# In the seventh attention turn GpSimd takes the low part of h ahead of the product with z; in the eighth VectorE makes w1's low parts ahead of the denominators

## The chip, the cores and the metric

One core of a Trainium2 chip runs the whole kernel as one launch. The metric is device time in microseconds (us) of that launch. The kernel before takes 517.39 us (median of 3 runs, 517.29 to 517.85).

## The reference

A transformer-like block over 2048 tokens of width 512, in float32. First comes linear attention with 32 heads of width 16, whose queries and keys pass through a small matrix per head and then a softmax of both signs; then a token-mixing MLP with 1792 hidden units that works along the token axis.

```python
qkv = layernorm(x) @ wqkv                                  # 32 heads of 16
pq, pk = per-head q @ w_phi, k @ w_phi
phi_q = concat(softmax(pq), softmax(-pq))
phi_k = concat(softmax(pk), softmax(-pk))
kv = sum over s of phi_k^T v ;  z = sum over s of phi_k
o = (phi_q kv) / (phi_q z + 1e-6)
h = x + o @ wo
n = layernorm(h)
u = gelu(einsum("sd,sf->df", n, w1) + b1)                  # w1: 2048 x 1792
out = h + einsum("df,fs->sd", u, w2) + b2                  # w2: 1792 x 2048
```

## The kernel before, in words

The tokens are cut into 16 tiles of 128. Matrix products that need float32 accuracy are made of three matmuls: each operand is split into a high part (rounded copy, made by ScalarE) and a low part (operand minus high part, made by VectorE or GpSimd), and `mm3` issues high by high (line 68), high by low (line 69) and low by high (line 70).

After keys and values are done, a loop of 20 turns (`for it in range(NT + 4)`, line 715) runs the query side of attention as a software pipeline, with the first two column pairs of the MLP's first product (`fills`, line 698) between its steps, so that TensorE always has something to do. Within the loop the order on TensorE, VectorE, ScalarE and GpSimd is the order in which the code is written; the queue of SyncE, which issues the loads, is ordered by a scheduler. An engine works its list strictly in order. The first turn is `it = 0`, so the seventh is `it = 6` and the eighth `it = 7`. What a turn does, by helper:

- `s_pq(it+1)` (GpSimd, line 473): multiplies the softmax numerators `eq` of a query tile by their weights `w`.
- `s_ez(it+3)` (GpSimd, line 457): `ez = eq * zB`, the product with z, which the denominators of that tile need.
- `s_den(it+2)` (VectorE, lines 466 to 470): sums `ez` per head into `tz`, combines it with the softmax sums `smq`, and ends in the weights `w` (line 470), which `s_pq` of the next turn uses.
- `q_sums` (VectorE, line 230): the softmax sums `smq` of one further query tile.
- `s_tr`, `s_num`, `s_wo` (TensorE lines 547, 566 and 68 to 70 with `po`): transposes, numerators and the product with wo. ScalarE copies the results out as `pht` (line 549) and `oh` (line 572), and VectorE makes `ol` (line 577).
- `s_h(it-2)` (VectorE, line 594): adds x, giving a tile of `h`.
- `s_moments`, `s_rstd`, `s_hn(it-4)` (ScalarE lines 603 to 605, GpSimd line 610 as `r`, ScalarE lines 613 to 63): the second layer norm. The last gives `hs`, whose high part ScalarE copies (line 63) and whose low part GpSimd subtracts (line 64). These are the names `hs<-hb,hs` in the profile.
- `fills(it)` (TensorE, lines 68 to 70 with `pu<-hs`): in turn `it` it first takes tile `it-6` of `hs` with column pair 1 of w1, then tile `it-5` with column pair 0, six matmuls each. The second and the fifth of the six (line 69) read the low part of `hs`, the third and the sixth (line 70) the low part of w1.
- `flush` (VectorE, line 664): makes the low parts `wlo` of those pieces of w1 whose high parts ScalarE has made (line 670). They wait in the list `LATER` until a `flush` comes.

The lines of a turn around the change:

```python
        if it < NT:
            s_x(it)
        if it + 3 < NT:
            s_ez(it + 3)
        negate()
        q_mm()
        fills(it)
        q_exp(0)
        logits = q_logits(1)
        if it >= 4 and even:
            s_hn(it - 4)
        ...
        run(logits + (q_sums(0) if it > 0 else []), den)
        ...
        if 0 <= it - 2 < NT:
            s_h(it - 2)
        flush()
```

`run` issues its two lists alternately. `negate` and `logits` have nothing left to do in the turns spoken of here, the logits of all 16 query tiles having been made before.

Of the kernel before, what the change touches and what calls it, by code (L numbers as in the profile page):

```python
# [19 lines left out]
NT = S // P  # L20
# [9 lines left out]
Q_AT = (4, 6, 8, 9, 11, 13)  # L30
V_NOT = (0, 1, 11)
SUMS = 8
DEN_EPS = 1e-6
LAG = 5
WARM = 9
# [4 lines left out]
def block_kernel(ctx: ExitStack, tc: tile.TileContext, x, xT, wT, phic, wo, w1, b1, w2, b2,  # L40
# [17 lines left out]
    nc.vector.memset(eps2[:, :1], EPS * EPS)  # L58
    nc.vector.memset(eps2[:, 1:], DEN_EPS / 2)

    def split(hi, lo, src, lo_engine):

        nc.scalar.activation(hi, src, AF.Copy)  # L63
        lo_engine.tensor_sub(lo, src, hi)  # L64
# [16 lines left out]
    ps_s = px.enter_context(tc.tile_pool(name="ps_s", bufs=1, space=PSUM, side="right"))  # L81
    sums = ps_s.tile([P, SUMS, NPR, 2, 2], F32, name="smq")
    wqp = aq.enter_context(tc.tile_pool(name="wqp", bufs=1, side="right"))
# [93 lines left out]
    def turns(*lists):  # L177

        return [ops[i] for i in range(max(map(len, lists))) for ops in lists if i < len(ops)]

    def run(*lists):
        for op in turns(*lists):
            op()
# [4 lines left out]
    def heads(e):  # L188
        return e.rearrange("p g (a d) -> p (g a) d", d=DH)
# [36 lines left out]
    def q_sum(t):  # L226

        assert t < SUMS or t - SUMS in W, "a tile's sums would go where others are still wanted"
        SQ[t] = sums[:, t % SUMS]
        return [lambda: nc.vector.reduce_sum(SQ[t].rearrange("p g c h -> p (g c h)"), heads(EQ[t]), axis=AX.X)]  # L230
# [144 lines left out]
    def q_mm():  # L375
        if q["mm"] < NT:
            PS[q["mm"]] = proj(q["mm"], wqh, wql, ps_q, "pu")
            q["mm"] += 1

    def q_logits(lag):  # L380
        n = q["logits"]
        if n < min(NT, q["mm"] - lag + NT * (q["mm"] == NT)):
            EQ[n] = big.tile([P, NG, P], F32, name="eq", tag="big")
            q["logits"] += 1
            return logit_ops(PS[n], EQ[n], n >= len(Q_AT))
        return []
# [7 lines left out]
    def q_sums(lag):  # L394
        n = q["sum"]
        if n < min(NT, q["exp"] - lag + NT * (q["exp"] == NT)):
            q["sum"] += 1
            return q_sum(n)
        return []
# [55 lines left out]
    def s_ez(t):  # L455
        EZ[t] = az.tile([P, NG, P], F32, name="ez")
        nc.gpsimd.tensor_mul(EZ[t], EQ[t], zB)  # L457

    def s_den(t):


        tz = az.tile([P, NPR, 2, 2], F32, name="tz")
        den = az.tile([P, NPR, 2], F32, name="den")
        W[t] = az.tile([P, NPR, 2, 2], F32, name="w", bufs=3)
        other = SQ[t][:, :, ::-1]
        return [lambda: nc.vector.reduce_sum(tz.rearrange("p g c h -> p (g c h)"), heads(EZ[t]), axis=AX.X),
                lambda: nc.vector.tensor_mul(tz, other, tz),
                lambda: nc.vector.reduce_sum(den, tz.rearrange("p g c h -> p g h c"), axis=AX.X),
                lambda: nc.vector.reciprocal(den, den),
                lambda: nc.vector.tensor_mul(W[t], other, den.unsqueeze(2).to_broadcast([P, NPR, 2, 2]))]  # L470

    def s_pq(t):
        nc.gpsimd.tensor_mul(heads(EQ[t]), heads(EQ[t]), W[t].rearrange("p g c h -> p (g c h)").unsqueeze(2).to_broadcast([P, 2 * H, DH]))  # L473
# [54 lines left out]
    def keep(shape, dt, name, i):  # L528
        return keep_pool.tile(shape, dt, name=name, tag=f"keep{i}")
# [11 lines left out]
    def s_tr(t):  # L541
        j, i = divmod(t, 2)
        if i == 0:
            PHT[j] = ak.tile([P, NG, 2, P], F32, name="pht", bufs=1)
        ptr = ps_t.tile([P, 2, 4, P], F32, name="tn")
        for g in range(NG):
            nc.tensor.transpose(ptr[:, g // 4, g % 4, :], EQ[t][:, g, :], ident)  # L547
        for half in range(2):
            nc.scalar.activation(PHT[j][:, half * 4:half * 4 + 4, i, :], ptr[:, half], AF.Copy)  # L549

    def s_kv():

        pt = ps_o.tile([P, 2, P], F32, name="po")
        for b in range(2):
            nc.tensor.transpose(pt[:, b, :], kvS[:, 2 * b:2 * b + 2, :].rearrange("p n f -> p (n f)"), ident)
        nc.scalar.activation(kvB, pt, AF.Copy)

    def s_num(j):


        pn = ps_t.tile([P, 2, 4, P], F32, name="tn")
        for b in range(2):
            for c in range(4):
                for r in range(2):
                    rows, cols = slice(64 * r, 64 * r + 64), slice(32 * c, 32 * c + 32)
                    nc.tensor.matmul(pn[cols, r, 2 * b:2 * b + 2, :], kvB[rows, b, cols], PHT[j][rows, 4 * b + c, :, :],
                                     start=True, stop=True, skip_group_check=True)
        oh = ak.tile([P, 2, 2, 2, P], F32R, name="oh", bufs=1)
        ol = ak.tile([P, 2, 2, 2, P], F32R, name="ol", bufs=1)
        pv = pn.rearrange("p r (b i) s -> p i r b s", i=2)  # L570
        for i in range(2):
            nc.scalar.activation(oh[:, i], pv[:, i], AF.Copy)
        OS[j] = oh, ol, pv
# [35 lines left out]
    def s_rstd(t):  # L609
        nc.gpsimd.tensor_tensor(r2[:, t:t + 1], VE[t][:, 0:1], mhalf[:, :1], op=ALU.pow)  # L610

    def s_hn(t):
        nc.scalar.activation(VE[t][:, 1:2], VE[t][:, 1:2], AF.Copy, scale=r2[:, t:t + 1])
        i, k = divmod(t, 2)
        if i not in HB:
            if i == 7:
                HB[i] = hb7
            else:
                both = keep([P, 2, 4, HD], F32, "hb", i // 2)
                BOTH[i // 2] = both  # L620
                HB[i], HB[i + 1 - i // 6] = both[:, 0], both[:, 1 - i // 6]
        hn = HB[i][:, 2 * k:2 * k + 2].rearrange("p h d -> p (h d)")
        nc.scalar.activation(hn, HT[t], AF.Identity, scale=r2[:, t:t + 1], bias=VE[t][:, 1:2])
        HN[t] = big.tile([P, 2, D], F32R, name="hs", tag="big")
        split(HN[t][:, 0], HN[t][:, 1], hn, nc.gpsimd)
# [35 lines left out]
    def flush():  # L661
        while LATER:
            wl_, raw, wh_ = LATER.pop(0)
            LO.append(nc.vector.tensor_sub(wl_, raw, wh_).ins)
# [42 lines left out]
    def t_at(it, place):  # L707
        for op in T_AT.get((it, place), "").split():
            i = int(op[1])
            if op[0] in "hl":  # L710
                (t_hi if op[0] == "h" else t_lo)(i)
            else:
                t_sums(i, "abcd".index(op[0]))

    for it in range(NT + 4):
        even = it % 2 == 0
        t_at(it, 0)
        if 0 <= it + 1 < NT:
            s_pq(it + 1)
        if it == 0:  # L720
            s_tr(0)
            s_kv()
        if it == 1:
            run(q_logits(0))
            q_mm()
            s_tr(1)
        if it > 1 and even and it <= NT:
            s_num(it // 2 - 1)
        t_at(it, 1)
        den = s_den(it + 2) if it + 2 < NT else []  # L730
        if it > 1 and even and it <= NT:
            ol = s_ol(it // 2 - 1)
            run(ol[:1] + den[:1] + ol[1:])
            den = den[1:]
        if it < NT:
            s_x(it)
        if it + 3 < NT:
            s_ez(it + 3)
        negate()
        q_mm()  # L740
        fills(it)
        q_exp(0)
        logits = q_logits(1)
        if it >= 4 and even:
            s_hn(it - 4)
        if 3 <= it < NT + 3 and even:
            s_moments(it - 3)
        if it > 1 and even and it - 2 < NT:
            s_wo(it - 2)
        if 1 < it < NT:  # L750
            s_tr(it)
        if it > 1 and not even and it - 2 < NT:
            s_wo(it - 2)
        if it >= 4 and not even:
            s_hn(it - 4)
        if 3 <= it < NT + 3 and not even:
            s_moments(it - 3)
        if 3 <= it < NT + 3:
            s_rstd(it - 3)
        run(logits + (q_sums(0) if it > 0 else []), den)  # L760
        if it > 0:
            negate()
        if not logits:
            flush()
        t_at(it, 2)
# [3 lines that stand above are left out]
        t_at(it, 3)  # L769
        if it > NT + 1:  # L770
            fill_load(2)
        for p in range(2):
            if it >= LAG - 3 + p and FL[p] <= FN[p] + 2 * (FN[p] > 0):
                fill_load(p)
# [488 lines left out]
```

## Time and profile before

| | |
|---|---|
| median of 3 runs | 517.39 us (517.29 to 517.85) |
| the profiled execution's own time | 516.99 us |
| its span in the profile | 515.2 us |
| TensorE matmul busy | 509.3 us, 99% of the span |
| TensorE weight load busy | 439.3 us, 85% |
| VectorE busy | 445.9 us, 87% |
| ScalarE busy | 297.2 us, 58% |
| GpSimd busy | 244.6 us, 47% |
| TensorE clock granted | 1.00 |

The profile is of one execution. A row of its timeline gives the start in us from the beginning of the span, the duration, engine, line, operation, output and inputs; a bracket at the end gives the idle time of the engine before the row and what ended it. PE is TensorE, DVE VectorE, ACT ScalarE, POOL GpSimd. Consecutive instructions overlap a little, so the spacing of starts tells what an instruction costs its engine. In the 20 us from 180 to 200, which hold the seventh, eighth and part of the ninth turn, TensorE is busy for 18.85 us, VectorE for 18.15, ScalarE for 15.02 and GpSimd for 19.44; in the 20 us ahead of them and the 20 behind them TensorE is busy throughout.

### The profile page before, as it was taken

What the parts mean: (1) busy time and instruction counts of PE and PEld (TensorE: products, weight loads), DVE (VectorE), ACT (ScalarE), POOL (GpSimd) and SP (SyncE); (2) the same over time, 40 slices, a digit from 0 to 9 for tenths busy, and PEclk for the clock granted to TensorE, in tenths of its full rate; (3) what the DMA queues carried; (4) which work ended last, traced back from release to release, by engine and by line L of the source; (5) the groups of instructions that cost most, each with busy time, mean ns of one, the idle gap of its engine ahead of it and who ended that gap; (6) DMA issues with size and microseconds to landing.
All of it is one profiled execution on the core that took longest, in us unless ns stands there. A gap on an engine that the chain in (4) does not pass through costs nothing.

```text
span 515.2 us, 9360 instructions
## 1 busy us (share of the span) xinstructions
PE 509.3 (99%) x3546; PEld 439.3 (85%) x3546; DVE 445.9 (87%) x765; ACT 297.2 (58%) x494; POOL 244.6 (47%) x188
## 2 busy tenths in 40 slices
PE   8999999999999999999999999999999999999997
PEld 8888888887877778777788899998888898899897
DVE  6793999986789998777796998989989899998985
ACT  6998954525245876668976643457753444444430
POOL 2579799984999999975343300000002212211220
PEclk9999999999999999999999999999999999999999
DMA  8844311000041324333322333374135688667833
GB/s 315 268 124 123 83 45 39 1 1 2 22 145 41 103 83 142 124 123 123 112 93 83 83 104 104 101 245 137 47 123 127 161 184 165 148 140 194 166 44 78
DMA packets 36300, 58.56 MB, mean 114 GB/s; under 512 B 3744, under 2 KB 19360, under 8 KB 36256
## 3 DMA queue, kind: packets, MB, share of 16 engines
q1 hardware_dynamic: 31648, 50.85, 31.5%
q0 software_dynamic: 4032, 6.42, 9.5%
q8 instruction: 28, 0.46, 0.4%
q10 hardware_dynamic: 576, 0.69, 0.4%
q14 instruction: 16, 0.13, 0.1%
HBM read 46.81 MB, written 11.14 MB: 112 GB/s over the span
## 4 chain that ended last, share of the span: by engine, by line
PE 94%; POOL 3%; ACT 1%; DVE 1%; issue 0%; POOLq 0%
PE py L1105 20%; PE pu L935 12%; PE pu L68 8%; PE pu L69 8%; PE pu L70 8%; PE py L1109 7%; PE pv L69 3%; PE pv L70 3%; PE pv L68 3%; PE pk_ps L68 3%; PE pk_ps L69 2%; PE pk_ps L70 2%; PE tn L547 2%; PE po L70 2%; PE po L69 2%; PE po L68 2%
## 5 line engine op out<-in xcount | busy, mean ns | idle before, releaser
L1181 POOL DMA_DIRECT2D out<-ot x7 | 6.2, 885 | 157.7 <-DVE ot L1177 157.7
L991 ACT ACTIVATE whi<-wraw 128x1792 fp32r<-128x1792 f32 x28 | 47.6, 1702 | 44.2 <-DVE wraw L858 26.6
L1001 DVE TENSOR_TENSOR wlo<-wraw,whi 128x1792 fp32r<-128x1792 f32 x28 | 56.6, 2020 | 4.9 <-PE py L1109 4.7
L1105 PE MATMUL py<-uf,whi 128*128 128x512 f32 x210 | 57.6, 393 | 0.0
L69 PE MATMUL pu<-hs,whi 128*128 128x512 f32 x128 | 50.3, 393 | 1.2 <-POOL hs L64 1.2
L68 PE MATMUL pu<-hs,whi 128*128 128x512 f32 x128 | 50.1, 399 | 0.0
L70 PE MATMUL pu<-hs,wlo 128*128 128x512 f32 x128 | 47.9, 390 | 0.0
L896 ACT ACTIVATE whi<-wraw 128x896 fp32r<-128x896 f32 x24 | 22.9, 955 | 31.2 <-PE pu L935 26.2
L457 POOL TENSOR_TENSOR ez<-eq,zB 128x1024 f32<-128x1024 f32 x16 | 38.3, 2396 | 4.5 <-ACT zB L502 4.5
L1105 PEld LDWEIGHTS py<-uf,whi 128*128 128x128 f32 x210 | 35.8, 189 | 4.3
L1105 PEld LDWEIGHTS py<-uf,wlo 128*128 128x128 f32 x210 | 33.1, 190 | 4.6
L935 PE MATMUL pu<-ht,whi 128*128 128x256 f32 x192 | 35.6, 283 | 0.0
L1105 PE MATMUL py<-uf,wlo 128*128 128x256 f32 x210 | 34.9, 280 | 0.0
L210 POOL TENSOR_TENSOR pk<-pk,sk 128x1024 f32<-128x1024 f32 x16 | 31.0, 1941 | 6.3 <-DVE sk L209 6.3
L64 POOL TENSOR_TENSOR hs<-hb,hs 128x512 fp32r<-128x512 f32 x16 | 22.3, 1393 | 24.4 <-ACT hs L63 24.3
L549 ACT ACTIVATE pht<-tn 128x512 f32<-128x512 f32 x32 | 17.4, 596 | 28.6 <-PE tn L547 28.4
L473 POOL TENSOR_TENSOR eq<-eq,w 128x1024 f32<-128x1024 f32 x16 | 32.2, 2013 | 0.8 <-DVE w L470 0.8
L214 POOL TENSOR_TENSOR zacc<-zacc,pk 128x1024 f32<-128x1024 f32 x13 | 31.2, 2402 | 0.6
L186 ACT ACTIVATE pk<-pk,r 128x1024 f32<-128x1024 f32 x16 | 18.3, 1146 | 21.1 <-DVE pk L164 21.1
L68 PEld LDWEIGHTS pu<-hs,whi 128*128 128x128 f32 x128 | 24.0, 188 | 7.1 <-issue 2.5
L935 PEld LDWEIGHTS pu<-ht,whi 128*128 128x128 f32 x192 | 30.0, 192 | 0.0
L69 PEld LDWEIGHTS pu<-hs,whi 128*128 128x128 f32 x128 | 24.1, 188 | 6.6 <-POOL hs L64 2.1
(208 smaller groups left out, 1606.6 us busy)
## 6 DMA issues: line engine op xcount, KB each, us to landing
wraw<-in_w SPq DMA_DIRECT2D x28, 512.0 KB, 4.2
wraw<-in_w SPq DMA_DIRECT2D x48, 256.0 KB, 2.8
xraw<-in_xT SPq DMA_DIRECT2D x16, 256.0 KB, 3.0
xh<-in_x SPq DMA_DIRECT2D x16, 256.0 KB, 2.7
h<-in_x SPq DMA_DIRECT2D x16, 256.0 KB, 2.8
out<-h SPq DMA_DIRECT2D x14, 256.0 KB, 2.7
out<-ot POOLq DMA_DIRECT2D x14, 256.0 KB, 4.9
wraw<-in_wT SPq DMA_DIRECT2D x12, 256.0 KB, 5.1
```

Of the source, the lines that this page charges most:

```text
L68: nc.tensor.matmul(o, ah, bh, start=first, stop=False)
L69: nc.tensor.matmul(o, ah, bl, start=False, stop=False)
L70: nc.tensor.matmul(o, al, bh, start=False, stop=last)
L210: nc.gpsimd.tensor_mul(heads(PK[t]), heads(PK[t]), sk.unsqueeze(2).to_broadcast([P, 2 * H, DH]))
L214: nc.gpsimd.tensor_add(zacc, zacc, PK[t])
L457: nc.gpsimd.tensor_mul(EZ[t], EQ[t], zB)
L473: nc.gpsimd.tensor_mul(heads(EQ[t]), heads(EQ[t]), W[t].rearrange("p g c h -> p (g c h)").unsqueeze(2).to_broadcast([P, 2 * H, DH]))
L935: nc.tensor.matmul(ACC[p][bk][:, half], WS[p, i][x][:, a], hb[b][y], start=i == 0 and half == 0 and k == 0, stop=i == NT // 2 - 1 and k == ...
L991: nc.scalar.activation(WH[g], RAW[g], AF.Copy)
L1001: nc.vector.tensor_sub(wl_, RAW[g], WH[g])
L1105: nc.tensor.matmul(o, w, u, start=p == 0 and not low, stop=p == NP - 1, skip_group_check=True)
L1109: nc.tensor.matmul(bank[bk][:, half], AW[sp, p][x][:, a], UB[p, b][:, y], start=p == 0 and half == 0 and i == 0, stop=p == NP - 1 and i == ...
```

## The change

It swaps two steps on GpSimd in the seventh turn and puts two steps of VectorE earlier in the eighth. No instruction is added or removed.

```diff
+TURN = 6
...
-        if it + 3 < NT:
+        if it + 3 < NT and it != TURN:
             s_ez(it + 3)
         negate()
         q_mm()
...
         if it >= 4 and even:
             s_hn(it - 4)
+        if it == TURN:
+            s_ez(it + 3)
         if 3 <= it < NT + 3 and even:
             s_moments(it - 3)
...
         if 3 <= it < NT + 3:
             s_rstd(it - 3)
+        if it == TURN + 1:
+            run(q_sums(0))
+            flush()
         run(logits + (q_sums(0) if it > 0 else []), den)
```

On GpSimd, in the seventh turn and the one after it: `eq_1571` is query tile 7, `ez_2223` (after: `ez_2243`) the product with z for tile 9, `hs_2242` (after: `hs_2240`) the low part of h's tile 2, `hs_2341` that of tile 3; `eq_1619` and `eq_1773` are query tiles 8 and 9. The list before:

```order
L473 TENSOR_TENSOR eq_1571<-eq_1571,w_2123 128x1024
L457 TENSOR_TENSOR ez_2223<-eq_1773,zB_1536 128x1024
L64 TENSOR_TENSOR hs_2242<-hb_2071,hs_2242 128x512
L610 TENSOR_TENSOR r2_68<-ve2_2185,mhalf_63 128x1
L473 TENSOR_TENSOR eq_1619<-eq_1619,w_2217 128x1024
L457 TENSOR_TENSOR ez_2300<-eq_1785,zB_1536 128x1024
L64 TENSOR_TENSOR hs_2341<-hb_2071,hs_2341 128x512
```

And after, where the numbers of the lines are one higher from the new constant on:

```order
L474 TENSOR_TENSOR eq_1571<-eq_1571,w_2123 128x1024
L65 TENSOR_TENSOR hs_2240<-hb_2071,hs_2240 128x512
L458 TENSOR_TENSOR ez_2243<-eq_1773,zB_1536 128x1024
L611 TENSOR_TENSOR r2_68<-ve2_2185,mhalf_63 128x1
L474 TENSOR_TENSOR eq_1619<-eq_1619,w_2217 128x1024
L458 TENSOR_TENSOR ez_2300<-eq_1785,zB_1536 128x1024
L65 TENSOR_TENSOR hs_2341<-hb_2071,hs_2341 128x512
```

Only the second and the third row have changed places; what follows, and every later turn, is as it was.

On VectorE, in the eighth turn: `h_2049` is the last step of the seventh, `smq` the softmax sums (of query tile 11 from `eq_1838`, of tile 12 from `eq_1900`), `tz_2295` to `w_2297` the denominators of tile 9, `wlo_2286` and `wlo_2291` the low parts of two pieces of w1, `h_2124` the turn's last step, `ol_2384` (after: `ol_2385`) the first of the ninth turn. Before:

```order
L594 SCALAR_TENSOR_TENSOR h_2049,ve2_2281<-po_2249,h_2049 128x512
L230 TENSOR_REDUCE smq_83<-eq_1838 128x64
L466 TENSOR_REDUCE tz_2295<-ez_2223 128x64
L467 TENSOR_TENSOR tz_2295<-smq_83,tz_2295 128x64
L468 TENSOR_REDUCE den_2296<-tz_2295 128x32
L469 RECIPROCAL den_2296<-den_2296 128x32
L470 TENSOR_TENSOR w_2297<-smq_83,den_2296 128x64
L664 TENSOR_TENSOR wlo_2286<-wraw_2284,whi_2285 128x512
L664 TENSOR_TENSOR wlo_2291<-wraw_2289,whi_2290 128x512
L594 SCALAR_TENSOR_TENSOR h_2124,ve2_2357<-po_2326,h_2124 128x512
L577 TENSOR_TENSOR ol_2384<-tn_2366,oh_2383 128x512
```

After:

```order
L595 SCALAR_TENSOR_TENSOR h_2049,ve2_2281<-po_2249,h_2049 128x512
L231 TENSOR_REDUCE smq_83<-eq_1838 128x64
L665 TENSOR_TENSOR wlo_2286<-wraw_2284,whi_2285 128x512
L665 TENSOR_TENSOR wlo_2291<-wraw_2289,whi_2290 128x512
L231 TENSOR_REDUCE smq_83<-eq_1900 128x64
L467 TENSOR_REDUCE tz_2295<-ez_2243 128x64
L468 TENSOR_TENSOR tz_2295<-smq_83,tz_2295 128x64
L469 TENSOR_REDUCE den_2296<-tz_2295 128x32
L470 RECIPROCAL den_2296<-den_2296 128x32
L471 TENSOR_TENSOR w_2297<-smq_83,den_2296 128x64
L595 SCALAR_TENSOR_TENSOR h_2124,ve2_2358<-po_2326,h_2124 128x512
L578 TENSOR_TENSOR ol_2385<-tn_2367,oh_2384 128x512
```

The two low parts stand ahead of the denominators, and since `q_sums` now runs twice in this turn, the sums of tile 12 come into it from the ninth; every later turn's sums come one turn earlier too, until the 16 tiles are used up. On TensorE and ScalarE nothing changes its place.

On SyncE, the scheduler puts two loads the other way round: `wraw_2616` (after: `wraw_2617`) is a piece of w1, `h_2298` the tile of x to which the tenth turn adds, `out_0` a store of h. Before:

```order
L596 DMA out_0<-h_2049 128x512
L669 DMA wraw_2523<-in_w1 128x2x256
L588 DMA h_2298<-in_x 128x512
L669 DMA wraw_2616<-in_w1 128x2x256
L596 DMA out_0<-h_2124 128x512
```

After:

```order
L597 DMA out_0<-h_2049 128x512
L670 DMA wraw_2524<-in_w1 128x2x256
L670 DMA wraw_2617<-in_w1 128x2x256
L589 DMA h_2298<-in_x 128x512
L597 DMA out_0<-h_2124 128x512
```

The load of w1 now stands ahead of the load of x.

## The prediction

> **What bounds the kernel now.** I read the page's chain first, then TensorE's waits.
>
> ```profile
> PE 94%; POOL 3%; ACT 1%; DVE 1%; issue 0%; POOLq 0%
> ```
>
> ```profile
> PE pu L69 <- POOL hs L64: 1.2, 1, 1.2
> ...
> PE po L70 <- DVE ol L577: 0.2, 1, 0.2
> ```
>
> TensorE is the bound: the chain that ended last is 94% TensorE. Once started, it waits long only once (columns: total, times, longest), for GpSimd's low part of h, so only that wait is to be won; what GpSimd or VectorE gain elsewhere is worth nothing by itself. TensorE's timeline shows the place, the eighth turn, and three later rows that I need as marks.
>
> ```profile
> 185.96 0.39 PE L68 MATMUL pu<-hs,whi 128*128 128x512 f32 x1
> 187.50 0.50 PE L69 MATMUL pu<-hs,whi 128*128 128x512 f32 x1 [1.15 <-POOL hs L64]
> 187.84 0.40 PE L70 MATMUL pu<-hs,wlo 128*128 128x512 f32 x1
> ...
> 194.06 0.39 PE L70 MATMUL pu<-hs,wlo 128*128 128x512 f32 x1
> ...
> 195.20 0.39 PE L69 MATMUL pu<-hs,whi 128*128 128x512 f32 x1
> 195.43 0.39 PE L70 MATMUL pu<-hs,wlo 128*128 128x512 f32 x1
> ...
> 201.76 0.39 PE L70 MATMUL pu<-hs,wlo 128*128 128x512 f32 x1
> ```
>
> Undisturbed matmuls start 0.23 us apart (195.20 to 195.43). After 185.96 the L70 would have started at 186.42; it started at 187.84. The wait costs **1.42 us**, more than the 1.15 in the bracket, since the pipeline has to fill again. That is the most the change can bring.
>
> GpSimd's timeline through these turns, two pieces of one list:
>
> ```profile
> 181.49 1.94 POOL L473 TENSOR_TENSOR eq<-eq,w 128x1024 f32<-128x1024 f32 x1
> 183.39 2.38 POOL L457 TENSOR_TENSOR ez<-eq,zB 128x1024 f32<-128x1024 f32 x1
> 185.73 1.72 POOL L64 TENSOR_TENSOR hs<-hb,hs 128x512 fp32r<-128x512 f32 x1
> 187.41 0.54 POOL L610 TENSOR_TENSOR r<-ve,mhalf 128x1 f32<-128x1 f32 x1
> 187.93 1.93 POOL L473 TENSOR_TENSOR eq<-eq,w 128x1024 f32<-128x1024 f32 x1
> 189.82 2.39 POOL L457 TENSOR_TENSOR ez<-eq,zB 128x1024 f32<-128x1024 f32 x1
> 192.69 1.81 POOL L64 TENSOR_TENSOR hs<-hb,hs 128x512 fp32r<-128x512 f32 x1 [0.48 <-ACT hs L63]
> 194.47 0.54 POOL L610 TENSOR_TENSOR r<-ve,mhalf 128x1 f32<-128x1 f32 x1
> 194.98 1.94 POOL L473 TENSOR_TENSOR eq<-eq,w 128x1024 f32<-128x1024 f32 x1
> 196.88 2.41 POOL L457 TENSOR_TENSOR ez<-eq,zB 128x1024 f32<-128x1024 f32 x1
> 199.24 1.28 POOL L64 TENSOR_TENSOR hs<-hb,hs 128x512 fp32r<-128x512 f32 x1
> 200.48 1.00 POOL L610 TENSOR_TENSOR r<-ve,mhalf 128x1 f32<-128x1 f32 x1
> ```
>
> The reader is to see that GpSimd has almost no gap: it is full here. The low part of tile 2 ends at 187.45 and TensorE's L70 follows 0.39 us behind it. The next two, of tiles 3 and 4, end at 194.50 and 200.52; with the same 0.39 their L70 could start at 194.89 and 200.91, and start at 195.43 and 201.76. So TensorE can come forward by only 0.54 and 0.85 us before it meets GpSimd again, unless these low parts come earlier too. This, not the 1.42, decides.
>
> VectorE and ScalarE in the same stretch:
>
> ```profile
> 184.40 1.92 DVE L664 TENSOR_TENSOR wlo<-wraw,whi 128x512 fp32r<-128x512 f32 x1
> 186.24 0.68 DVE L594 SCALAR_TENSOR_TENSOR h<-po,h 128x512 f32<-128x512 f32 x1
> ...
> 186.85 1.22 DVE L230 TENSOR_REDUCE smq<-eq 128x64 f32<-128x1024 f32 x1
> 187.98 1.21 DVE L466 TENSOR_REDUCE tz<-ez 128x64 f32<-128x1024 f32 x1
> ...
> 190.12 0.22 DVE L470 TENSOR_TENSOR w<-smq,den 128x64 f32<-128x64 f32 x1
> 190.26 3.10 DVE L664 TENSOR_TENSOR wlo<-wraw,whi 128x512 fp32r<-128x512 f32 x2
> 193.28 0.68 DVE L594 SCALAR_TENSOR_TENSOR h<-po,h 128x512 f32<-128x512 f32 x1
> ...
> 195.41 0.69 DVE L577 TENSOR_TENSOR ol<-tn,oh 128x512 fp32r<-128x512 f32 x1 [1.44 <-ACT oh L572]
> ...
> 200.04 1.03 DVE L664 TENSOR_TENSOR wlo<-wraw,whi 128x512 fp32r<-128x512 f32 x1
> ```
>
> ```profile
> 181.84 0.63 ACT L63 ACTIVATE hs<-hb 128x512 fp32r<-128x512 f32 x1
> ...
> 185.75 1.15 ACT L670 ACTIVATE whi<-wraw 128x512 fp32r<-128x512 f32 x2
> ...
> 189.83 1.09 ACT L549 ACTIVATE pht<-tn 128x512 f32<-128x512 f32 x2 [1.89 <-PE tn L547]
> ...
> 191.98 0.63 ACT L63 ACTIVATE hs<-hb 128x512 fp32r<-128x512 f32 x1
> ...
> 194.31 1.07 ACT L572 ACTIVATE oh<-tn 128x512 fp32r<-128x512 f32 x2
> ```
>
> A low part of w1 and GpSimd hold each other up. The one issued at 184.40 goes through only when GpSimd's running product is over: VectorE's next instruction starts at 186.24, 0.51 us after GpSimd's boundary at 185.73. GpSimd's instruction behind that boundary then takes 1.72 instead of 1.28; likewise the r at 200.48, 1.00 instead of 0.54. So a low part costs GpSimd about 0.45 us. For two in a row the nearest place is another pair of VectorE subtractions of this shape, with the same instructions behind the boundary:
>
> ```profile
> 234.93 2.06 DVE L634 TENSOR_TENSOR hb<-hb 128x512 f32<-128x512 f32 x2
> ```
>
> ```profile
> 235.70 0.97 POOL L610 TENSOR_TENSOR r<-ve,mhalf 128x1 f32<-128x1 f32 x1
> 236.65 2.15 POOL L473 TENSOR_TENSOR eq<-eq,w 128x1024 f32<-128x1024 f32 x1
> ```
>
> The first costs the r 0.43 (0.97 against 0.54), the second the product behind it 0.21 (2.15 against 1.94), and the second ends 0.78 after the first (236.99 less 236.21, the boundary plus 0.51).
>
> **The change part by part.** *GpSimd, seventh turn.* The low part of tile 2 starts at 183.39, where the product with z started; its high part is there (181.84 + 0.63 = 182.47). It takes 1.24 us of GpSimd (199.24 to 200.48) and is over by 184.67, well ahead of the 186.19 at which TensorE wants it. The wait of 1.42 us goes.
>
> *What is late next: the low part of tile 3.* GpSimd's list, with the spacings of the rows above: 183.39 + 1.24 (low part) = 184.63; + 2.34 (183.39 to 185.73, ez) + 0.45 (the low part of w1 issued at 184.40) = 187.42; r 0.52 + 0.45 = 188.39; product with w 1.89 + 0.21 = 190.49; ez 2.36 (196.88 to 199.24) = 192.85; low part 1.28 = 194.13. Its high part doesn't hold it: ScalarE's chain from 189.83 to 191.98 starts on a TensorE transpose, so it comes up to 1.42 earlier. TensorE's L70 then starts at 194.13 + 0.39 = 194.52 where it started at 195.43: **0.91 us** are left, and 0.51 of the 1.42 are given back. Bounds: with no cost for the second of the pair 1.12; with the full 0.45 for it 0.67.
>
> *Then tile 4.* From 192.85: 1.24 + 0.51 (r, 194.47 to 194.98) + 1.90 + 2.36 = 198.86, and the low part ends at 200.14, or at 200.59 if the ninth turn's low part of w1 lands ahead of it. That one was issued at 200.04; its chain goes back through ol (195.41) and oh (194.31) to the same transpose, so it comes at 200.04 - 1.42 = 198.62, just ahead of 198.86, and hits. L70 starts at 200.98 instead of 201.76: 0.78 left; without the hit still 0.91. From the tenth turn on I take the low parts of h to wait for ScalarE, which waits for TensorE, so all move together, and the rest of the kernel, in which TensorE waits for nothing but the 0.2 us for ol above, moves up whole.
>
> *VectorE, eighth turn.* The low part issued at 184.40 gets through at 184.63 + 0.51 = 185.14, earlier than before, so h goes at 185.14, smq at 185.75 and the first moved low part at 186.88 (spacings 0.61 and 1.13). Its inputs are there (whi, 185.75 + 1.15). It passes at 187.42 + 0.51 = 187.93, the second at 188.71. TensorE needs that one at 194.06 - 1.42 = 192.64: covered by 3.9 us. In the old order the pair ended at 193.28, which would have held TensorE; this is what the second edit takes away. Behind the pair stand the extra smq (1.13, to 189.84), tz to w (2.14 + 0.22) and h. The weights w of tile 9 are ready at 192.2, 1.9 us later than before (190.34); GpSimd asks for them at 194.60, so 2.4 us cover it. The delayed ez of tile 9 is ready at 187.4, 2.4 us before tz. VectorE then waits for oh until 194 as it did before (1.44 us idle), so the extra smq costs nothing, and later turns have one each as before.
>
> *SyncE.* The load of w1 that now precedes a load of x may go when the second low part is made, 188.7 instead of 193.3; the x tile behind it is not read before the tenth turn. Cost nothing; if held, no more than a load's landing, far ahead of its use.
>
> **The sum.** 1.42 - 0.51 - (0 to 0.13) = 0.78 to 0.91; I take 0.85. The profiled execution of 516.99 us (span 515.2, 1.8 around it) would come to 516.1; the median of 517.39 to **516.5**. By the bounds of the second low part the gain is 0.55 to 1.12. A gain of 0.2% (1.03 us, about what a measurement of this kernel can tell from no change) lies inside these bounds, so the sum alone cannot tell a small gain from none that is seen.
>
> **The rivals.** *The whole wait goes.* If the low parts of w1 held up GpSimd less than the rows say, tile 3 would be ready sooner: without any of the three holds at 194.13 - 1.11 = 193.02, L70 undisturbed at 194.01, and all 1.42 stay: 516.0. For it: some 0.12 us less than my sum already passes 1.03. Against: the 0.45 shows at two places.
>
> *The second low part is shut out for a whole product.* Then it waits from 187.93 until the product with w is over, at 188.39 + 1.89 = 190.28, and ez takes 0.45 instead of the 0.21 before it: tile 3 ends at 194.37, gain 0.67, w is ready at 194.3, just in time, and the ninth turn's low part of w1 comes too late to hit tile 4: 516.7. Against it: at 234.93 the second of the pair went through at once. The Trainium skill, "SBUF — State Buffer", section "Who interferes with whom", states such a rule: a VectorE instruction with two SBUF inputs and a GpSimd instruction that reads SBUF share a read port as an exclusive lock, which the first to issue keeps for the whole instruction. The trace agrees that VectorE waits a product out (1.92 us at 184.40); that GpSimd loses only 0.45 is less than a whole block.
>
> *Slower: the denominators become the wait.* In the eighth turn w of tile 9 now stands behind two low parts and one more sum. From 194.60 on, each us that w is later delays the product with w, ez and the low part of tile 4 by one us. From about 195.4 the gain is gone; at 196.6 the kernel is 1.2 us slower, 518.6. It would take low parts of 3 us each. Against: the 3.10 us for two at 190.26 hold 2 us of waiting for one product, and from 186.88 another product ends within 0.54.
>
> **How the numbers follow.** The sum with its bounds 0.54, of which I put 0.19 above a gain of 1.03 and 0.35 below; the whole wait 0.22; the shut-out low part 0.10; slower 0.14. Faster: 0.19 + 0.22 = 0.41. Within 0.2%: 0.35 + 0.10 = 0.45. Slower: 0.14. The range goes from the whole wait less the scatter of the median (516.0 - 0.2) to no gain at all, 517.4; it leaves out the slower case and little else. The likeliest case alone spans 516.3 to 516.8.
>
> **What would show it.** TensorE's wait for hs in the eighth turn is gone, and a shorter one, of 0.3 to 0.6 us, stands in the ninth, for the low part of tile 3; perhaps a mark of 0.1 in the tenth. GpSimd's r after ez takes about 1.0 and the product behind it 2.1. The product with w of tile 9 waits for nothing. I am wrong if the ninth turn shows no wait, if GpSimd waits there for VectorE's w, or if TensorE waits for ol or wlo.

## The result, and the profile after

The changed kernel takes 516.63 us (median of 20 runs, 516.14 to 517.07), the kernel before 517.55 in the same session (20 runs, 516.94 to 518.24). The ratio is 0.9983, with a 95% interval of 0.9976 to 0.9989: 0.92 us faster. The interval lies wholly below 1, so there is a gain; it also holds the 0.2% that I had called distinguishable, so a gain of that size is not ruled out.

TensorE's part of the waits view, after (total, times, longest):

```profile
PE pk_ps L303 <- DVE eps L60: 1.1, 1, 1.1
PE pu L283 <- DVE wraw L273: 0.4, 1, 0.4
PE pv L283 <- DVE wraw L273: 0.4, 1, 0.4
...
PE po L71 <- DVE ol L578: 0.2, 1, 0.2
PE pu L70 <- POOL hs L65: 0.2, 1, 0.2
```

The wait of 1.2 us for the low part of h is gone and one of 0.2 stands in its place. The two rows `L283 <- L273` stand at the start of the kernel, where the first loads arrive: VectorE waits there 1.07 us for a piece of the weights, which it doesn't in the profile of before. They are not the change's. TensorE is already 0.61 us late at 10.35 us (a matmul that starts at 9.74 before), the eighth turn starts 0.60 us later than in the profile of before, and this is why the two spans, 515.2 and 515.0, differ by less than the medians. So I read the gain inside the kernel, between two marks: the first matmul on w1 of the eighth turn and that of the eleventh. TensorE's timeline, before:

```profile
184.50 0.48 PE L68 MATMUL pu<-hs,whi 128*128 128x512 f32 x1
...
207.40 0.50 PE L68 MATMUL pu<-hs,whi 128*128 128x512 f32 x1
```

And after, with the places between the marks where TensorE isn't on time:

```profile
185.10 0.48 PE L69 MATMUL pu<-hs,whi 128*128 128x512 f32 x1
...
194.14 0.39 PE L69 MATMUL pu<-hs,whi 128*128 128x512 f32 x1
194.69 0.50 PE L70 MATMUL pu<-hs,whi 128*128 128x512 f32 x1 [0.16 <-POOL hs L65]
195.03 0.40 PE L71 MATMUL pu<-hs,wlo 128*128 128x512 f32 x1
...
201.16 0.50 PE L70 MATMUL pu<-hs,whi 128*128 128x512 f32 x1
201.50 0.40 PE L71 MATMUL pu<-hs,wlo 128*128 128x512 f32 x1
...
207.15 0.50 PE L69 MATMUL pu<-hs,whi 128*128 128x512 f32 x1
```

22.90 us before, 22.05 after: 0.85 us are won. At 0.23 us a matmul the L71 after 194.14 would have started at 194.60; it starts at 195.03, so 0.43 are given back in the ninth turn. In the tenth, L71 comes 0.34 behind L70 instead of 0.23: 0.11 more. Of the 1.42 us of the old wait that leaves 0.88, against 0.85 between the marks; where the other 0.03 go I leave open. To the last numerators, `tn<-pht`, which start at 248.12 before and 247.87 after, it is 0.85 still: nothing is lost behind the eleventh turn.

GpSimd's timeline after shows what the 0.43 and the 0.11 are:

```profile
183.99 1.28 POOL L65 TENSOR_TENSOR hs<-hb,hs 128x512 fp32r<-128x512 f32 x1
185.23 2.86 POOL L458 TENSOR_TENSOR ez<-eq,zB 128x1024 f32<-128x1024 f32 x1
188.05 0.99 POOL L611 TENSOR_TENSOR r<-ve,mhalf 128x1 f32<-128x1 f32 x1
189.02 2.03 POOL L474 TENSOR_TENSOR eq<-eq,w 128x1024 f32<-128x1024 f32 x1
191.00 2.38 POOL L458 TENSOR_TENSOR ez<-eq,zB 128x1024 f32<-128x1024 f32 x1
193.35 1.29 POOL L65 TENSOR_TENSOR hs<-hb,hs 128x512 fp32r<-128x512 f32 x1
...
195.12 1.94 POOL L474 TENSOR_TENSOR eq<-eq,w 128x1024 f32<-128x1024 f32 x1
...
199.36 1.75 POOL L65 TENSOR_TENSOR hs<-hb,hs 128x512 fp32r<-128x512 f32 x1
```

The low part of tile 2 is over at 185.27, long before TensorE asks. Tile 3's ends at 194.64, and 0.39 later, at 195.03, L71 starts. Tile 4's is held (1.75 instead of 1.28) and ends at 201.11; L71 starts at 201.50, again 0.39 later. VectorE's timeline has the instructions that hold it:

```profile
185.05 0.77 DVE L665 TENSOR_TENSOR wlo<-wraw,whi 128x512 fp32r<-128x512 f32 x1
...
187.48 1.76 DVE L665 TENSOR_TENSOR wlo<-wraw,whi 128x512 fp32r<-128x512 f32 x2
189.16 1.21 DVE L231 TENSOR_REDUCE smq<-eq 128x64 f32<-128x1024 f32 x1
...
192.43 0.22 DVE L471 TENSOR_TENSOR w<-smq,den 128x64 f32<-128x64 f32 x1
192.57 0.68 DVE L595 SCALAR_TENSOR_TENSOR h<-po,h 128x512 f32<-128x512 f32 x1
194.58 0.69 DVE L578 TENSOR_TENSOR ol<-tn,oh 128x512 fp32r<-128x512 f32 x1 [1.32 <-ACT oh L573]
...
199.21 0.74 DVE L665 TENSOR_TENSOR wlo<-wraw,whi 128x512 fp32r<-128x512 f32 x1
```

The low part at 185.05 makes the ez 2.86 instead of 2.38, the pair at 187.48 makes the r 0.99 and the product behind it 2.03, and the one at 199.21 lands on tile 4. The weights w are made by 192.65, and GpSimd asks for them at 195.12, without a wait.

### The profile page after: what moved, and what is told of

It is laid out like the page before. It is cut to its first block, busy times and chain, and to the rows that moved or that the text cites. A ratio compares the mean times of both kernels' runs of the same rounds, so it can differ in the third digit from the quotient of the medians.

```text
span 515.0 us, 9359 instructions
## 1 busy us (share of the span) xinstructions
PE 509.3 (99%) x3546; PEld 438.9 (85%) x3546; DVE 445.6 (87%) x765; ACT 297.7 (58%) x494; POOL 244.8 (48%) x188
## 4 chain that ended last, share of the span: by engine, by line
PE 82%; POOL 11%; DVE 2%; ACT 2%; issue 1%; DMA 1%; SPq 0%; POOLq 0%
PE py L1111 20%; PE pu L941 12%; PE py L1115 7%; PE pu L69 7%; PE pu L70 6%; PE pu L71 6%; POOL ez L458 5%; POOL eq L474 3%; PE pv L70 3%; PE pk_ps L69 3%; PE pk_ps L70 2%; PE pk_ps L71 2%; PE pv L71 2%; PE pv L69 2%; POOL eq L176 2%; PE po L71 2%
## 5 line engine op out<-in xcount | busy, mean ns | idle before, releaser
L70 PE MATMUL pu<-hs,whi 128*128 128x512 f32 x128 | 50.4, 394 | 0.2 <-POOL hs L65 0.2
L71 PE MATMUL pu<-hs,wlo 128*128 128x512 f32 x128 | 47.9, 390 | 0.0
L70 PEld LDWEIGHTS pu<-hs,whi 128*128 128x128 f32 x128 | 24.1, 188 | 5.8 <-POOL hs L65 1.4
```

What stands on the lines that cost most here:

```text
L70: nc.tensor.matmul(o, ah, bl, start=False, stop=False)
L71: nc.tensor.matmul(o, al, bh, start=False, stop=last)
```

## The experiments

Each was timed against the kernel before on the same chip, and its profile was read between the same marks. "Gain" is what a kernel needs less than before between them; the last column goes from the first mark to the last numerators (63.62 us before).

| kernel | us | before | ratio (95%) | gain to the 11th turn | gain to the last numerators |
|---|---|---|---|---|---|
| e1_swap_only | 517.16 | 517.13 | 0.9997 (0.9988 to 1.0005) | 0.40 | 0.40 |
| e2_flush_only | 518.44 | 517.13 | 1.0024 (1.0015 to 1.0034) | -1.25 | -1.24 |
| e3_swap_two_turns | 517.54 | 517.13 | 1.0004 (0.9995 to 1.0013) | 0.02 | 0.03 |
| e4_swap_to_the_end | 516.29 | 517.13 | 0.9985 (0.9976 to 0.9993) | 1.24 | 0.80 |
| e5_tiles_2_and_4 | 516.70 | 517.20 | 0.9984 (0.9975 to 0.9993) | 0.98 | 0.98 |
| e6_tiles_2_3_4 | 516.55 | 517.20 | 0.9985 (0.9976 to 0.9993) | 1.24 | 0.87 |
| e7_pair_as_memsets | 515.87 | 517.20 | 0.9973 (0.9962 to 0.9984) | 1.44 | 1.44 |
| e8_tiles_2_3_4_flush | 516.40 | 517.20 | 0.9985 (0.9976 to 0.9993) | 1.44 | 0.90 |
| e9_end_and_h_first | 516.00 | 517.38 | 0.9972 (0.9962 to 0.9982) | 1.44 | 1.44 |
| e10_after_again | 516.54 | 517.38 | 0.9985 (0.9976 to 0.9994) | 0.83 | 0.82 |

**e1: the first edit alone.** The three lines of the eighth turn are left out:

```diff
-        if it == TURN + 1:
-            run(q_sums(0))
-            flush()
```

> Only the swap on GpSimd; VectorE's eighth turn as before. Mark: from the eighth turn's first matmul on w1 to the eleventh's, 22.90 us before, 22.05 with the whole change (gain 0.85). Theory (the second edit is needed): the pair of low parts of w1 is issued at about 189.8, behind the denominators, meets a product of GpSimd and ends at about 193.3 where TensorE wants it at 192.6; the wait goes over to w1's low part, gain 0.3 to 0.6, mark 22.3 to 22.6. Rival (the swap alone does it): the pair slips through ahead of the next product, gain 0.85, mark 22.05.

GpSimd, VectorE and TensorE around the ninth turn of e1:

```profile
190.84 2.88 POOL L458 TENSOR_TENSOR ez<-eq,zB 128x1024 f32<-128x1024 f32 x1
```

```profile
190.78 3.48 DVE L665 TENSOR_TENSOR wlo<-wraw,whi 128x512 fp32r<-128x512 f32 x2
```

```profile
193.35 0.40 PE L70 MATMUL pu<-hs,whi 128*128 128x512 f32 x1
194.32 0.50 PE L71 MATMUL pu<-hs,wlo 128*128 128x512 f32 x1 [0.58 <-DVE wlo L665]
```

The pair of w1's low parts comes, as in the old order, behind the denominators. Its first gets through at 190.84, at the boundary between two instructions of GpSimd; its second has to wait until the ez behind that boundary is over (3.48 us for the two), and TensorE, 1.42 us earlier than before, waits for it: 0.74 us to this matmul and 0.11 to the next. That leaves 0.57. Another 0.17 goes in the tenth turn, where tile 4's low part is held too (1.74 at 200.15) and comes a little late for TensorE. The swap alone is worth 0.40.

**e2: the second edit alone.** GpSimd's order is that of before; VectorE has the three lines that e1 leaves out.

> Only the second edit: VectorE's low parts of w1 and the extra sums ahead of the denominators, GpSimd's order as before. Theory: the 1.42 us wait for the low part of h in the eighth turn stays, nothing else is late, gain 0 within 0.2, mark 22.9. Rival (the low parts of w1 were what TensorE really waited for): gain 0.5 or more, mark 22.4 or less. A loss would show as GpSimd waiting for the weights w of tile 9.

It is slower by 0.24%, which I had not expected: I had priced this edit at nothing. GpSimd's, VectorE's and TensorE's rows:

```profile
188.22 1.93 POOL L473 TENSOR_TENSOR eq<-eq,w 128x1024 f32<-128x1024 f32 x1
190.11 2.84 POOL L457 TENSOR_TENSOR ez<-eq,zB 128x1024 f32<-128x1024 f32 x1
...
197.06 1.94 POOL L473 TENSOR_TENSOR eq<-eq,w 128x1024 f32<-128x1024 f32 x1 [1.90 <-DVE w L470]
```

```profile
188.26 5.24 DVE L664 TENSOR_TENSOR wlo<-wraw,whi 128x512 fp32r<-128x512 f32 x2
...
196.69 0.22 DVE L470 TENSOR_TENSOR w<-smq,den 128x64 f32<-128x64 f32 x1
196.84 0.68 DVE L594 SCALAR_TENSOR_TENSOR h<-po,h 128x512 f32<-128x512 f32 x1
```

```profile
187.79 0.50 PE L69 MATMUL pu<-hs,whi 128*128 128x512 f32 x1 [1.16 <-POOL hs L64]
...
197.67 0.47 PE L68 MATMUL po<-woh,oh 128*128 128x512 f32 x1 [0.85 <-DVE h L594]
```

The pair is issued at 188.26, just after a product began at 188.22. The first low part waits that product out, the second the whole ez behind it: 5.24 us for two instructions that take 1.76 in the changed kernel. Denominators, w and h behind them are late; GpSimd waits 1.90 for w and TensorE 0.85 for h, with the old wait still in place. This is the mechanism of my slower rival and of the shut-out one together: the prediction had them at 0.14 and 0.10 for the whole change, and both happen here, where a long ez and not the short r stands behind the boundary at which the pair gets through. So the edits don't add up (0.40 and -1.25 alone, 0.85 together): the swap sets where in GpSimd's list the pair falls.

**e3: the swap in the seventh and the eighth turn** (`ez` goes behind the low parts of tiles 2 and 3).

```diff
+SWAP = (6, 7)
...
-        if it + 3 < NT and it != TURN:
+        if it + 3 < NT and it not in SWAP:
             s_ez(it + 3)
...
-        if it == TURN:
+        if it in SWAP and even:
             s_ez(it + 3)
...
         if it >= 4 and not even:
             s_hn(it - 4)
+        if it in SWAP and not even:
+            s_ez(it + 3)
```

> The whole change, and the product with z behind the low part of h in the eighth turn too. The scheduler also swaps some later instructions (at 350 to 385 us). Theory (GpSimd is full and only the order of its list decides who waits): tile 3 is ready early and the wait of the ninth turn is gone, but tile 4 is late by GpSimd's wait for the high part of tile 3, the tenth turn waits 1.0 to 1.4 us, gain 0 to 0.45, mark 22.45 to 22.9. Rival (the give-back in the ninth turn is a matter of tile 3 alone): gain 1.3, mark 21.6.

TensorE's only wait between the marks in e3:

```profile
201.39 0.50 PE L71 MATMUL pu<-hs,whi 128*128 128x512 f32 x1 [1.13 <-POOL hs L66]
```

The wait is as long as the old one (1.13 against 1.15 in the bracket) and stands two tiles of h further on: all that was won is lost again in the tenth turn. Getting one low part forward puts its ez in front of another one.

**e4: the swap in every turn from the seventh to the thirteenth** (`SWAP = (6, 7, 8, 9, 10, 11, 12)` in e3's code).

> The whole change, and the product with z behind the low part of h in every turn from the seventh to the thirteenth. Theory: all low parts of h come ahead of what TensorE wants, the whole 1.42 us is kept, mark 21.5, time 1.4 us below before. Rival (without GpSimd's low parts TensorE meets VectorE next, for ol or for denominators that now come late): a wait for ol or for eq stands in the tenth to twelfth turn, gain 0.9 or less.

No wait for the low part of h is left, but the full 1.42 us are not kept: 0.18 are lost in the tenth turn, which leaves 1.24 to the eleventh, and 0.44 in the twelfth. VectorE and TensorE in e4:

```profile
198.88 2.56 DVE L666 TENSOR_TENSOR wlo<-wraw,whi 128x512 fp32r<-128x512 f32 x1
201.36 0.68 DVE L596 SCALAR_TENSOR_TENSOR h<-po,h 128x512 f32<-128x512 f32 x1
...
213.23 2.57 DVE L666 TENSOR_TENSOR wlo<-wraw,whi 128x512 fp32r<-128x512 f32 x1
215.72 0.68 DVE L596 SCALAR_TENSOR_TENSOR h<-po,h 128x512 f32<-128x512 f32 x1
```

```profile
202.10 0.50 PE L70 MATMUL po<-woh,oh 128*128 128x512 f32 x1
...
216.47 0.50 PE L70 MATMUL po<-woh,oh 128*128 128x512 f32 x1 [0.16 <-DVE h L596]
```

A low part of w1 now meets an ez that has just begun and waits 2.56 us, and the h behind it releases TensorE's product with wo too late, a little at 202.10 (h ends at 202.04) and more at 216.47. VectorE's order is the next bound.

**e5 and e6: tiles 2 and 4, and tiles 2, 3 and 4** (`SWAP = (6, 8)` and `(6, 7, 8)`).

> The whole change, and in the ninth turn too (not in the eighth) the low part of h, tile 4, goes ahead of the product with z. Theory: the ninth turn's wait for tile 3 stays (0.43 lost there), only the small one of the tenth goes, gain 0.98, mark 21.9. Rival: a low part of w1 then waits for the product with z and holds up h, gain below 0.85.

> The whole change, and the low part of h ahead of the product with z in the eighth and the ninth turn too. Theory: as in the kernel that swaps to the end up to the eleventh turn (gain 1.24, mark 21.66), and since the later turns keep the old order, nothing is given back behind it: gain 1.24 to the end, time 1.2 us below before. Rival: the fuller order costs later turns in another way, and 0.4 is given back in the twelfth as there.

In e5 the tenth turn's 0.11 comes back and the ninth turn's wait stays (a bracket of 0.17 for `hs`, as after); the 0.98 are kept. So the tenth turn's loss can be taken away by itself, as in the prediction's sum. In e6 both are gone; the tenth turn loses 0.18 as in e4, for the same h (201.41, behind a low part of 2.55), so 1.24 us are won, but 0.37 are given back behind the eleventh turn. GpSimd's rows there:

```profile
206.12 1.75 POOL L66 TENSOR_TENSOR hs<-hb,hs 128x512 fp32r<-128x512 f32 x1
...
212.59 1.75 POOL L66 TENSOR_TENSOR hs<-hb,hs 128x512 fp32r<-128x512 f32 x1
```

These are tiles 5 and 6. In the kernel before, GpSimd waits 0.87 us for ScalarE ahead of tile 5, and a low part of w1 gets through in that gap; in e6, with TensorE and so ScalarE a good microsecond earlier, the gap is closed and the low part holds up the `hs` itself. They put TensorE back by 0.19 and 0.15 us, counted against e5's matmuls from the same numerators on, which is 0.34 of the 0.37.

**e7: what the pair costs GpSimd.** The changed kernel, with zeros written in place of the eighth turn's two low parts (they are left out of the computation):

```diff
-    def flush():
+    def flush(empty=False):
         while LATER:
             wl_, raw, wh_ = LATER.pop(0)
+            if empty:
+                nc.vector.memset(wl_.bitcast(F32), 0.0)
+                continue
             LO.append(nc.vector.tensor_sub(wl_, raw, wh_).ins)
...
         if it == TURN + 1:
             run(q_sums(0))
-            flush()
+            flush(True)
```

> The whole change with the two low parts of w1 that were put forward replaced by memsets of zeros, which read no memory (so the two low parts are left out of the products). Theory (the subtractions with two operands in SBUF hold GpSimd up): the r in the eighth turn takes 0.54 instead of 0.99, the product behind it 1.94 instead of 2.03, tile 3's low part is 0.5 earlier, the ninth turn's wait is gone, gain 1.3 to 1.42, mark 21.5 to 21.6. Rival (GpSimd is late by its own list alone): r stays at 0.99, gain 0.85, mark 22.05.

GpSimd in e7, from the ez on:

```profile
184.91 2.87 POOL L458 TENSOR_TENSOR ez<-eq,zB 128x1024 f32<-128x1024 f32 x1
187.73 0.56 POOL L611 TENSOR_TENSOR r<-ve,mhalf 128x1 f32<-128x1 f32 x1
188.25 1.95 POOL L474 TENSOR_TENSOR eq<-eq,w 128x1024 f32<-128x1024 f32 x1
190.15 2.40 POOL L458 TENSOR_TENSOR ez<-eq,zB 128x1024 f32<-128x1024 f32 x1
192.50 1.30 POOL L65 TENSOR_TENSOR hs<-hb,hs 128x512 fp32r<-128x512 f32 x1
```

r takes 0.56 instead of 0.99, the product 1.95 instead of 2.03. Tile 3 is over 8.98 us behind the first mark (9.54 in the changed kernel), and no wait is left in the ninth turn. Tile 4 comes early enough too, ahead of the next low part of w1, which then holds up only the r behind it. The gain is 1.44, the whole of the old wait: what the change gives back is the hold of the pair on GpSimd, 0.51 us by these two rows, and the tenth turn's loss that follows from it. The Trainium skill, "SBUF — State Buffer", section "Who interferes with whom", has VectorE contend with GpSimd's reads by instructions with two SBUF inputs, and not by those with one input at most, outside VectorE's 2-port modes. Here the subtractions hold GpSimd and the memsets in their place don't (r 0.99 against 0.56), so the trace agrees.

**e8: e6, and the ninth turn's low part of w1 ahead of the denominators too.**

```diff
         if it == TURN + 1:
             run(q_sums(0))
+        if it in (TURN + 1, TURN + 2):
             flush()
```

> As the kernel with tiles 2, 3 and 4 put ahead, and in the ninth turn the low part of w1 stands ahead of the softmax sums and denominators too. Theory: that low part no longer waits for a whole product with z, h is in time for the product with wo in the tenth turn, gain 1.42, mark 21.48, time 1.4 us below before. Rival: w of tile 10 comes too late for GpSimd, gain 1.2 or less.

To the eleventh turn the gain is the full 1.44; behind it 0.54 are given back at the same tiles 5 and 6, whose low parts take 1.76 and 1.79 us. By the time it is no better than e6.

**e9 and e10: e4 with h ahead of the low part of w1, beside the changed kernel.** In the ninth, eleventh and thirteenth turn h goes first:

```diff
+        if it in (8, 10, 12):
+            s_h(it - 2)
         if not logits:
             flush()
         t_at(it, 2)
-        if 0 <= it - 2 < NT:
+        if 0 <= it - 2 < NT and it not in (8, 10, 12):
             s_h(it - 2)
```

> As e4 (ez behind the low part of h from the seventh turn to the thirteenth, the pair of w1's low parts ahead in the eighth), and in the ninth, eleventh and thirteenth turn VectorE adds h ahead of the low part of w1. Theory: what e4 gave back (0.18 us in the tenth turn, 0.44 in the twelfth) was h standing behind a low part that waited for a whole product with z; with h ahead of it both losses go and the 1.42 us are kept to the end. From the start of the eighth turn's w1 matmuls to the eleventh's 21.5 us (22.90 before, 21.66 in e4), to the last numerators 62.2 (63.62, 62.82). Time 515.7 to 515.9, 1.3 to 1.4 under the kernel before. Rival: the low part of w1, now later by the 0.6 of an h, or what stands behind it, is late for TensorE: then a wait for wlo or w appears in the tenth or twelfth turn and the gain stays at 0.8 to 1.2.

> The changed kernel once more, unaltered, on the same chip as e9, for a direct comparison. The gain is 0.85 us again by the marks (22.05 and 62.77), the time 0.8 to 1.0 under the kernel before; by the theory e9 is 0.5 to 0.6 us faster than this one, by the rival within 0.3 of it.

VectorE and GpSimd in e9:

```profile
200.47 0.68 DVE L596 SCALAR_TENSOR_TENSOR h<-po,h 128x512 f32<-128x512 f32 x1
...
201.07 1.96 DVE L666 TENSOR_TENSOR wlo<-wraw,whi 128x512 fp32r<-128x512 f32 x1
```

```profile
192.76 1.29 POOL L66 TENSOR_TENSOR hs<-hb,hs 128x512 fp32r<-128x512 f32 x1 [0.80 <-ACT hs L65]
...
206.68 1.52 POOL L66 TENSOR_TENSOR hs<-hb,hs 128x512 fp32r<-128x512 f32 x1 [1.32 <-ACT hs L65]
...
220.59 1.28 POOL L66 TENSOR_TENSOR hs<-hb,hs 128x512 fp32r<-128x512 f32 x1 [1.09 <-ACT hs L65]
```

h no longer stands behind the low part that waits, TensorE waits for nothing from the eighth turn to the last numerators, and GpSimd waits for ScalarE at tiles 3, 5 and 7, as it did before (0.48, 0.87 and 1.73 us), while TensorE no longer waits for it. The full 1.44 us are kept: 516.00 against 517.38, 0.28% faster than before. Against the changed kernel on the same chip (516.54) it is 0.54 us less, which is what the marks say (62.18 against 62.80 to the last numerators); the two ratios' intervals overlap, so by the times alone e9 is not shown to be the faster of the two.

## Why the prediction was right

- *The wait goes.* As worked out: no wait for `hs` in the eighth turn.
- *Tile 3 in the ninth turn takes part of it back.* Forecast 0.51 us, measured 0.43. The term that was off is the cost of the second low part of the pair, for which I took 0.21 from another pair: the product behind it takes 2.03 instead of 1.94, so 0.09. That other pair ended 1.29 us behind its boundary (235.70 to 236.99), this one 1.19 (188.05 to 189.24); why is open. The first one's 0.45 was right (r 0.99 against 0.54). The sign that I gave, a wait of 0.3 to 0.6, holds for what the wait costs; its bracket is 0.16. e7 shows that without the pair's holds nothing is given back.
- *Tile 4 in the tenth.* Forecast 0 to 0.13, with the ninth turn's low part of w1 hitting it; it does, and costs 0.11. e5 shows that this loss can be taken away with the ninth turn's left as it is; e7, that it also goes when tile 3 comes earlier.
- *VectorE.* The pair gets through together, as forecast (1.76 us); w is ready 2.47 us before GpSimd asks, against 2.4 forecast. In e1 the second edit's purpose shows: the pair in its old place costs TensorE 0.85 us.
- *The sum.* 0.85 us, measured 0.85 between the marks and 0.92 by the medians; the time forecast was 516.5 us, measured 516.63. That the two 0.85 agree to the hundredth is luck: 0.85 was the middle between a tenth turn that loses nothing and one that loses 0.13. It did lose, by which my sum would have been 0.78, and the 0.08 too much that I had taken for the ninth turn made up for it.
- *The rivals.* The whole wait goes when the pair's two holds on GpSimd are taken away: e7, where the third hold, on the ez (2.87), is still there. The shut-out low part and the late denominators did not happen here, but e1 and e2 show both as real, with e2 at +1.3 us. I had put the 14% on low parts of 3 us each; what kept the pair short here was, as I read it, not the length of a low part but the short r behind the boundary. I had this from the order of the list alone, without the case in which it fails, so my price for the second edit by itself, nothing, was wrong by 1.25 us.
- *SyncE.* No wait for a load appeared in the turns concerned.

## What to carry to other kernels

Where a full engine feeds the bound one, taking a wait away brings the bound forward only to that engine's next due time: list the next few due times before pricing the wait. Two subtractions on VectorE beside products on GpSimd took 1.8 us or 5.2 us here, by when they were issued and by what GpSimd ran behind the boundary where the first got through. I would put such a pair where a short instruction of GpSimd follows, and what TensorE needs soon should stand ahead of it. Two edits of an order should be tried apart as well as together: here one alone is a loss, and the pair a gain.

## What the runs showed of the hardware that was not expected

- The length of one and the same pair of VectorE subtractions (128x512 each): 1.76 us with the r behind the boundary, 3.48 with an ez behind it, 5.24 when it was issued just after a product began and an ez stood behind. Counted from the boundary at which the first gets through, the pair ends 1.19, 3.42 and 3.39 us later. The eight executions with the r behind the boundary (after, e3 to e6 and e8 to e10) all have 1.76 or 1.77. In all of these executions GpSimd's instruction behind the boundary lost only 0.4 to 0.5 us. I read this as one subtraction getting in at each boundary, the second at once only if the instruction behind the boundary is short; no run varied the length of that instruction by itself, so this reading is argued and not shown.
- A short wait of TensorE costs more than the idle time in its bracket, by about the same amount whatever its length: brackets of 1.15 (before), 1.13 (e3), 0.58 (e1) and 0.16 us (after) go with 1.42, 1.40, 0.85 and 0.43 us by the starts of the matmuls, 0.27 more each. The wait for h in e2 is not of this kind (0.85 and about 1.2). A matmul that is too little late for a bracket costs something as well: 0.11 in the tenth turn.
- The eighth turn, ahead of which nothing differs in its work, began at 184.69 and 185.10 us in two profiled executions of the changed kernel, and between 184.42 and 186.11 in the ten of other kernels; where the waits view names a cause (`L283 <- L273`, above), it is the first loads. A change of 1 us can't be read from two spans, but it can from two marks in the traces: the changed kernel's two executions agree there within 0.03 us.
